# First-pass stores of split weights over GpSimd's DMA queue, in a kernel that converts later stages' weights in pairs of units

## The chip, the cores and the metric

One NeuronCore of one Trainium2 chip runs the kernel. The time is device microseconds of one execution, and the median of three is given. One more execution was profiled. Engines are called as the profile calls them: PE (TensorE matmul), PEld (its weight load), DVE (VectorE), ACT (ScalarE), POOL (GpSimd) and SP (SyncE, which here only issues DMAs).

## The reference

Attention over 4 batches of 12 heads (448 positions, head size 64, q and k normalised first), then two MLPs on the 1792 x 768 result.

```python
q_n, k_n = rmsnorm(q, g_q), rmsnorm(k, g_k)
scores = scale * np.matmul(q_n, k_n.transpose(0, 1, 3, 2))
attn = softmax(scores)                               # rows
x = np.matmul(attn, v)                               # -> 1792 x 768
y = ((x @ w_a) * (x @ w_b)) @ w_out                  # 768 -> 1536 -> 768
h = y @ w2_in                                        # 768 -> 2048
g = np.maximum(h, 0) + alpha * np.minimum(h, 0)
out = g @ w2_out                                     # 2048 -> 768
```

The five weight matrices come from HBM with 8 bytes an element.

## The kernel before

**Stages.** The MLPs run for each batch b as four stages: a (both first matrices, product of the two), y, h and o. The list `stages` begins a0 y0 h0 o0 a1 y1 ... The attention of the later batches is cut into small steps, and a rate per stage says how many steps are put between two units of weights. The attention of batch 0 runs alone before a0.

**Units.** A unit is 128 columns of a weight matrix. Every f32 product is made of three f16 products (high x high, high x low, low x high), so each weight is stored as a high and a low f16 half. The first time a unit is used it goes through four steps, some units ahead of its matmuls: `w_load` brings the 8-byte elements into `raw` (three buffers), `w_convert` makes f32 of them (`wf`, lines 806 to 820), `w_scale` finds a power of two from their squares (`tot`, `pw`), and `w_split` writes the halves into `w16` (three buffers; ACT writes the high half, DVE the low one). `w_split` also stores `w16` to HBM, to `sc_a`, `sc_y`, `sc_h` or `sc_o`; later stages of the same kind load the halves from there with no conversion (`w<-sc_a`, from about 425 us). Stage a stores each unit by itself (line 880, 24 stores of 384 KB); y, h and o store two units at a time (line 888).

**What else is on SP.** All loads of q, k, v and weights, the stores of lines 880 and 888, the stores of the result (line 1279), and the attention's transposes. For a pair of heads these are `qT` and `kT` (lines 354, 357), two copies `qS<-qT` (lines 360, 361) that wait for `qT` to land, and then seven `pT<-p` (line 489) of the probabilities. The matmuls `s<-kT,qT` and `s<-kT,qS` are the scores, `x<-pT,v` the product with the values. There is one buffer for `pT`: the first `pT` of a pair of heads waits until `x<-pT,v` of the pair before has read it.

**What sets the order.** A scheduler puts the instructions of each engine into one fixed order from the dependencies and its own estimates; each engine, and SP's queue, then runs its list in that order. An instruction that waits holds up all behind it on its engine. Matmuls of line 110 are all issued by one helper.

**POOL** has only a few small instructions before 392 us; later it loads and stores blocks from which combined weights are made (`form_block`, lines 673 and 705).

Of the kernel before, what the change touches and what calls it, by code (L numbers as in the profile page):

```python
# [19 lines left out]
def attention_gated_mlps_kernel(  # L20
# [15 lines left out]
    nc = tc.nc  # L36
# [676 lines left out]
    stream, pairs_of = [], []  # L713
# [8 lines left out]
    scratch, raws, wf, w16 = {}, {}, {}, {}  # L722
# [17 lines left out]
    def size(kind):  # L740
        return CHAINS[kind][2] * 128

    def views(t, n):
        return t.rearrange("p u l n -> p (u l n)")[:, 0:4 * n].rearrange("p (u l n) -> p u l n", u=2, l=2)

    def w_half():
        return wh_p.tile([128, 2, 2, 768], F16, tag="w16", name="w16")
# [118 lines left out]
    def w_split(u):  # L866
        if u not in scales:
            return
        t, s = wf.pop(u), scales.pop(u)
        n = size(stream[u][0])  # L870
        if stream[u][0] == "a":
            w = half16.pop(u) if u in half16 else views(w_half(), n)
            if u in members:
                half16[u + 1] = w
            w16[u] = w = w[:, u % 2]
            nc.scalar.activation(out=w[:, 0], in_=t, func=AF.Copy, scale=s)
            nc.vector.scalar_tensor_tensor(
                out=w[:, 1], in0=t, scalar=s, in1=w[:, 0], op0=ALU.mult, op1=ALU.subtract
            )
            nc.sync.dma_start(out=scratch[stream[u]], in_=w)  # L880
            return
        w = views(w_half(), n)
        t = t.rearrange("p (u n) -> p u n", u=2)
        nc.scalar.activation(out=w[:, :, 0], in_=t, func=AF.Copy, scale=s)
        nc.vector.scalar_tensor_tensor(  # L885
            out=w[:, :, 1], in0=t, scalar=s, in1=w[:, :, 0], op0=ALU.mult, op1=ALU.subtract
        )
        nc.sync.dma_start(out=whole[stream[u]], in_=w)
        for j, x in enumerate(members[u]):
            w16[x] = w[:, j]  # L890


    STEPS = [(w_load, 10), (w_convert, 8), (w_scale, 6), (w_split, 3)]
    AGAIN = [(w_load, 4)]
    cur = [0]
# [528 lines left out]
```

## Time and profile before

| | |
|---|---|
| runs | 1214.96, 1218.82, 1220.37 us; median 1218.82 |
| profiled execution | 1218.45 us, of which the span of the profile is 1216.5 us |
| busy in the span | PE 94%, DVE 67%, ACT 62%, PEld 54%, POOL 9% |
| DMA | 269.75 MB, mean 222 GB/s; SP's queue 246.40 MB, POOL's queue 22.10 MB |
| granted clock of PE | mean 0.983 of 2.4 GHz |

The span is the time between the first and the last instruction; the profiled execution is 1.95 us longer than it. PE is the engine with the least idle time, so its idle time and the stretches at half clock are where time can be won or lost.

### The profile page before, as it was taken

What the parts mean: (1) busy time and instruction counts of PE and PEld (TensorE: products, weight loads), DVE (VectorE), ACT (ScalarE), POOL (GpSimd) and SP (SyncE); (2) the same over time, 40 slices, a digit from 0 to 9 for tenths busy, and PEclk for the clock granted to TensorE, in tenths of its full rate; (3) what the DMA queues carried; (4) which work ended last, traced back from release to release, by engine and by line L of the source; (5) the groups of instructions that cost most, each with busy time, mean ns of one, the idle gap of its engine ahead of it and who ended that gap; (6) DMA issues with size and microseconds to landing.
All of it is one profiled execution on the core that took longest, in us unless ns stands there. A gap on an engine that the chain in (4) does not pass through costs nothing. (4 is left out here: it accounts for less than half of the span.)

```text
span 1216.5 us, 19623 instructions
## 1 busy us (share of the span) xinstructions
PE 1146.1 (94%) x7168; PEld 655.1 (54%) x7168; DVE 810.6 (67%) x1647; ACT 758.8 (62%) x1439; POOL 113.9 (9%) x176
## 2 busy tenths in 40 slices
PE   5997999799988899898999999999999999999997
PEld 3553555345544444444445554454555558996597
DVE  7888999789998764777745366554456677523631
ACT  6998999898998865667534366564245335513532
POOL 1000000000000100000012110122300572000000
PEclk9998999899999899999999999999999999999999
DMA  7557999999999999888794587798833797864455
GB/s 192 163 178 187 282 330 325 301 270 321 309 273 296 281 242 238 208 217 187 193 215 161 154 184 159 191 220 200 226 130 124 249 300 237 278 217 145 149 175 164
DMA packets 297280, 269.75 MB, mean 222 GB/s; under 512 B 176704, under 2 KB 261184, under 8 KB 297184
## 3 DMA queue, kind: packets, MB, share of 16 engines
q1 hardware_dynamic: 289392, 246.40, 74.2%
q0 software_dynamic: 7792, 22.10, 6.2%
q8 instruction: 56, 0.92, 0.3%
q14 instruction: 40, 0.33, 0.1%
HBM read 179.77 MB, written 43.25 MB: 183 GB/s over the span
## 5 line engine op out<-in xcount | busy, mean ns | idle before, releaser
L110 PEld LDWEIGHTS <-w 128*128 128x128 f16 x4776 | 463.0, 99 | 403.2 <-issue 52.2
L110 PE MATMUL p<-x,w 128*128 128x448 f16 x1728 | 338.5, 354 | 6.8 <-DVE ab L1141 4.6
L110 PE MATMUL p<-y,w 128*128 128x448 f16 x1152 | 221.0, 353 | 0.8 <-DVE y L952 0.8
L110 PE MATMUL p<-ab,w 128*128 128x448 f16 x648 | 129.4, 359 | 3.2 <-ACT ab L951 3.2
L110 PE MATMUL p<-g,w 128*128 128x448 f16 (+1 forms) x588 | 120.2, 359 | 2.9 <-DVE w L885 1.7
L483 DVE SCALAR_TENSOR_TENSOR p<-pf,ri,p 128x448 f16<-128x448 f32 x126 | 84.4, 681 | 38.9 <-ACT p L482 38.8
L482 ACT ACTIVATE p<-pf,ri 128x448 f16<-128x448 f32 x126 | 81.2, 664 | 43.1 <-DMA pT<-p 34.3
L420 DVE TENSOR_REDUCE nm<-s 128x2 f32<-128x896 f32 x84 | 91.1, 1085 | 22.3 <-PE s L110 22.3
L437 ACT ACTIVATE pf<-s,nm,esc 128x448 f32<-128x448 f32 x126 | 90.1, 719 | 1.5
L110 PEld LDWEIGHTS <-ws 128*128 128x128 f16 x714 | 68.5, 98 | 0.4
L1144 ACT ACTIVATE junk<-ab 128x448 uint8<-128x448 f32 x48 | 27.5, 573 | 58.8 <-DVE ab L1141 58.7
L806 ACT ACTIVATE wf<-raw 128x768 f32<-128x768 f32 (+2 forms) x50 | 57.7, 1165 | 8.0 <-DMA raw<-in_moe_w_out_dram 6.5
L812 DVE SCALAR_TENSOR_TENSOR wf<-raw,wf 128x768 int32<-128x768 int32 (+2 forms) x50 | 61.9, 1241 | 0.2
L705 POOL DMA_DIRECT2D f_o_S<-raw x48 | 33.9, 821 | 283.1 <-DVE raw L701 205.2
L820 ACT ACTIVATE junk<-wf 128x768 uint8<-128x768 f32 (+2 forms) x50 | 53.9, 1078 | 6.2 <-DVE wf L812 2.7
L110 PE MATMUL s<-kT,qT 128*64 128x448 f16 x252 | 47.7, 372 | 10.0 <-DMA kT<-k 7.4
L1141 DVE SCALAR_TENSOR_TENSOR ab<-p,inv_a,t 128x448 f32<-128x448 f32 x48 | 32.5, 677 | 26.5 <-PE p L110 26.2
L110 PE MATMUL s<-early 128*128 128x448 f32 x84 | 40.3, 602 | 9.8 <-ACT pf L437 9.2
L110 PE MATMUL l<-g,ws 128*128 128x224 f16 x480 | 49.6, 259 | 0.0
L110 PE MATMUL l<-g,w 128*128 128x224 f16 x480 | 49.4, 259 | 0.0
L673 POOL DMA_DIRECT2D raw<-sc_o x48 | 37.6, 986 | 121.2 <-DMA raw<-in_moe_w_out_dram 71.8
L110 PE MATMUL s<-kT,qS 128*64 128x448 f16 x252 | 46.4, 357 | 1.5 <-DMA qS<-qT 1.5
(175 smaller groups left out, 1529.0 us busy)
## 6 DMA issues: line engine op xcount, KB each, us to landing
w<-sc_a SPq DMA_DIRECT2D x36, 768.0 KB, 5.0
w<-sc_h SPq DMA_DIRECT2D x24, 768.0 KB, 4.3
raw<-in_moe_w_in_dram SPq DMA_DIRECT2D x16, 768.0 KB, 8.4
raw<-in_moe_w_out_dram SPq DMA_DIRECT2D x24, 512.0 KB, 6.9
raw<-in_moe_w_a_dram SPq DMA_DIRECT2D x12, 768.0 KB, 6.2
raw<-in_moe_w_b_dram SPq DMA_DIRECT2D x12, 768.0 KB, 6.9
sc_a<-w SPq DMA_DIRECT2D x24, 384.0 KB, 6.8
raw<-in_moe_w_out_dram SPq DMA_DIRECT2D x12, 768.0 KB, 9.0
```

Of the source, the lines that this page charges most:

```text
L110: nc.tensor.matmul(out=o, lhsT=a, rhs=b, start=first, stop=last)
L420: nc.vector.tensor_reduce(out=nm, in_=ps[:, :, 0:S], axis=AX.X, op=ALU.max, negate=True)
L437: nc.scalar.activation(out=pf, in_=ps[:, j, 0:S], func=AF.Exp, bias=nm[:, j:j + 1], scale=scale[j], accum_out=su[:, j:j + 1],)
L482: nc.scalar.activation(out=t[:, 0, :, 0:KP], in_=pf, func=AF.Copy, scale=r)
L483: nc.vector.scalar_tensor_tensor(out=t[:, 1, :, 0:KP], in0=pf, scalar=r, in1=t[:, 0, :, 0:KP], op0=ALU.mult, op1=ALU.subtract,)
L673: tc.keep_in_program_order(nc.gpsimd.dma_start(out=x[:, q], in_=s))
L705: nc.gpsimd.dma_start(out=formed[kind, i, name, j][:, :, cols], in_=d["x"][:, q])
L806: nc.scalar.activation(out=t, in_=hi.bitcast(F32), func=AF.Prelu, scale=2.0 ** -112, alpha=-(2.0 ** 32))
L812: nc.vector.scalar_tensor_tensor(out=ti, in0=lo, scalar=29, in1=ti, op0=ALU.logical_shift_right, op1=ALU.bitwise_or)
L820: nc.scalar.activation(out=junk(1536, t.shape[1]), in_=t, func=AF.Square, accum_out=sums[0][:, j:j + 1])
L1141: nc.vector.scalar_tensor_tensor(out=ab, in0=ps, scalar=i, in1=t, op0=ALU.mult, op1=ALU.mult)
L1144: nc.scalar.activation(out=junk(1536, S), in_=ab, func=AF.Square, accum_out=ssab[:, b % 2, f:f + 1],)
```

## The change

The store at line 880 is issued by POOL in place of SP. Its source, its destination and its size are the same.

```diff
@@ -877,7 +877,7 @@  in w_split
             nc.vector.scalar_tensor_tensor(
                 out=w[:, 1], in0=t, scalar=s, in1=w[:, 0], op0=ALU.mult, op1=ALU.subtract
             )
-            nc.sync.dma_start(out=scratch[stream[u]], in_=w)
+            nc.gpsimd.dma_start(out=scratch[stream[u]], in_=w)
             return
```

The 24 stores stand on POOL between its load of `al` and its first `cum` operation, with nothing between them. Since the scheduler makes a new order, other instructions change places too: on PE between rows 95 and 3315 of some 13000, that is from about 117 us to about 445 us; behind that the order is the same.

The first place is SP's queue at the end of a0. The rows before, where `raw_2519` is the last unit of `w_out` and `pT_2290` belongs to the attention of batch 1:

```order
L880 DMA sc_a22_0_1976<-w16_2417 128x1536
L888 DMA sc_y0_0_2079<-w16_2492 128x3072
L778 DMA raw_2519<-in_moe_w_out_dram 128x6x128
L489 DMA_TRANSPOSE pT_2290<-p16_1_110 128x8x128
L489 DMA_TRANSPOSE pT_2290<-p16_2_111 128x8x128
L778 DMA raw_2519<-in_moe_w_out_dram 128x6x128
L489 DMA_TRANSPOSE pT_2290<-p16_3_112 128x8x128
```

The same place in the changed kernel:

```order
L366 DMA vn_3773<-in_v_dram 112x2x256
L778 DMA raw_2519<-in_moe_w_out_dram 128x6x128
L888 DMA sc_y0_0_2079<-w16_2492 128x3072
L778 DMA raw_2519<-in_moe_w_out_dram 128x6x128
L778 DMA raw_2690<-in_moe2_w_in_dram 128x6x128
L888 DMA sc_y1_0_2178<-w16_2602 128x3072
L489 DMA_TRANSPOSE pT_2290<-p16_1_110 128x8x128
```

The second half of `raw_2519` stood behind two `pT`; it now stands ahead of them.

The second place is SP's queue in y0. Before, `qT_2975` and `kT_2978` (the next pair of heads) stood behind the last `pT_2290` and behind the first two `pT_2933`:

```order
L489 DMA_TRANSPOSE pT_2290<-p16_3_112 128x8x128
L778 DMA raw_2858<-in_moe2_w_in_dram 128x6x128 x2
L888 DMA sc_y4_0_2445<-w16_2917 128x3072
L778 DMA raw_2953<-in_moe2_w_in_dram 128x6x128 x2
L489 DMA_TRANSPOSE pT_2933<-p16_0_109 128x8x128
L489 DMA_TRANSPOSE pT_2933<-p16_1_110 128x8x128
L354 DMA_TRANSPOSE qT_2975<-q16_2836 128x7x128
L357 DMA_TRANSPOSE kT_2978<-k16_2838 128x8x112
```

In the changed kernel they come ahead of the last two `pT_2290`:

```order
L489 DMA_TRANSPOSE pT_2290<-p16_1_110 128x8x128
L778 DMA raw_2764<-in_moe2_w_in_dram 128x6x128 x2
L354 DMA_TRANSPOSE qT_2975<-q16_2836 128x7x128
L357 DMA_TRANSPOSE kT_2978<-k16_2838 128x8x112
L206 DMA kr_2987<-in_k_dram 112x2x256
L210 DMA qr_2986<-in_q_dram 128x448
L360 DMA qS_2980<-qT_2975 64x896
L361 DMA qS_2980<-qT_2975 64x896
L778 DMA raw_2858<-in_moe2_w_in_dram 128x6x128
L489 DMA_TRANSPOSE pT_2290<-p16_2_111 128x8x128
L888 DMA sc_y3_0_2359<-w16_2823 128x3072
L489 DMA_TRANSPOSE pT_2290<-p16_3_112 128x8x128
```

Two more pairs are moved in the same way, ahead of the first two `pT` of their own heads: `qT_4073` in o0 and `qT_4854` at the end of o0. On PE, the scores and the `x<-pT,v` around them stand earlier by 3 to some 30 matmuls of weights.

The third place is PE in o0, at the unit `w_4468`. Before, 21 matmuls of that unit, the 24 of `x<-pT,v_4081` and two more of the unit stood ahead of the first score of the next heads:

```order
L110 MATMUL x<-pT,v_4081 64x448
L110 LDWEIGHTS w_4468
L110 MATMUL p<-g_13_3903,w_4468 128x448
L110 LDWEIGHTS w_4468
L110 MATMUL p<-g_15_3989,w_4468 128x448
L110 LDWEIGHTS qT
L110 MATMUL s<-kT,qT 64x448
```

In the changed kernel the 24 come first, then 12 matmuls of the unit, and then eight scores in a row:

```order
L110 MATMUL p<-g_14_3947,w_4468 128x448
L110 LDWEIGHTS qT
L110 MATMUL s<-kT,qT 64x448
L110 LDWEIGHTS qT
L110 MATMUL s<-kT,qT 64x448
L110 LDWEIGHTS qS
L110 MATMUL s<-kT,qS 64x448
```

The scores moved ahead of 11 matmuls; on SP the items ahead of this `qT` and `kT` are the same ones as before.

## Rows read from the trace of the kernel before

**Rows 1.** The page, busy time of each engine.

```profile
PE 1146.1 (94%) x7168; PEld 655.1 (54%) x7168; DVE 810.6 (67%) x1647; ACT 758.8 (62%) x1439; POOL 113.9 (9%) x176
```

**Rows 2.** Stretches: length, busy time per engine, granted clock, DMA share, GB/s.

```profile
120.00:210.00 90.00, 90.00 (x523) 48.74 (x519) 85.89 (x188) 87.78 (x166) 0.00 (x0) 1.00 1.08 306
...
200.00:220.00 20.00, 16.35 (x108) 8.90 (x105) 16.85 (x25) 17.17 (x26) 0.00 (x0) 1.00 1.05 318
220.00:240.00 20.00, 14.83 (x63) 7.42 (x63) 15.97 (x32) 16.61 (x29) 0.19 (x1) 0.74 1.11 313
...
400.00:420.00 20.00, 16.60 (x86) 7.83 (x83) 13.47 (x25) 14.13 (x26) 0.60 (x1) 0.83 1.14 272
```

**Rows 3.** Line 880: issues (ns min/median/max, first and last start), landing.

```profile
L880 SPq DMA_DIRECT2D sc_a<-w x24: 339/527/3517, 87.6 to 201.9; - x24
...
DMA to landing us min/median/max: 2.8/6.8/12.1
```

**Rows 4.** Timeline of PE in a0: start, length, line, instruction, count.

```profile
138.35 3.56 PE L110 MATMUL p<-x,w 128*128 128x448 f16 x18
```

**Rows 5.** Timeline of POOL, first instruction after its loads at the start.

```profile
223.70 0.19 POOL L1286 TENSOR_TENSOR cum<-ix,iab 128x1 f32<-128x1 f32 x1 [214.24 <-DVE iab L123]
```

**Rows 6.** Line 673, POOL's loads: ns min/median/max, first and last start.

```profile
L673 POOL DMA_DIRECT2D raw<-sc_o x48: 720/989/1299, 392.8 to 951.2; - x48
```

**Rows 7.** Timeline of SP's queue around the end of a0.

```profile
201.87 3.52 SPq L880 DMA_DIRECT2D sc_a<-w  x1
205.48 0.38 SPq L888 DMA_DIRECT2D sc_y<-w  x1
...
214.46 3.36 SPq L489 DMA_TRANSPOSE pT<-p  x2
217.87 0.58 SPq L778 DMA_DIRECT2D raw<-in_moe_w_out_dram  x1
```

**Rows 8.** Timeline of ACT before y0; in brackets idle time and its releaser.

```profile
223.49 1.58 ACT L806 ACTIVATE wf<-raw 128x1536 f32<-128x1536 f32 x1 [1.65 <-DMA raw<-in_moe_w_out_dram]
...
225.66 1.78 ACT L951 ACTIVATE ab<-ab,sab 128x448 f16<-128x448 f32 x3
```

**Rows 9.** Timeline of PE at four places from y0 to o0.

```profile
226.38 2.02 PE L110 MATMUL p<-ab,w 128*128 128x448 f16 x5 [3.18 <-ACT ab L951]
...
256.84 2.46 PE L110 MATMUL x<-pT,v 112*64 112x448 f16 x24 [0.56 <-DVE pw L117]
...
267.02 0.38 PE L110 MATMUL s<-kT,qT 128*64 128x448 f16 x2 [1.42 <-DMA kT<-k]
...
404.21 0.58 PE L110 MATMUL s<-kT,qT 128*64 128x448 f16 x2 [3.40 <-DMA kT<-k]
```

**Rows 10.** PE's waits, 240 to 445 us: total, times, longest.

```profile
PE s L110 <- DMA kT<-k: 7.4, 4, 3.4
...
PE s L110 <- DMA qS<-qT: 1.5, 2, 0.9
```

**Rows 11.** Timeline of SP's queue in y0.

```profile
242.50 2.66 SPq L489 DMA_TRANSPOSE pT<-p  x1
...
259.33 2.62 SPq L489 DMA_TRANSPOSE pT<-p  x2
262.00 1.49 SPq L354 DMA_TRANSPOSE qT<-q  x1
263.54 1.29 SPq L357 DMA_TRANSPOSE kT<-k  x1
...
266.75 0.59 SPq L361 DMA_DIRECT2D qS<-qT  x1
```

**Rows 12.** Landing of `kT`, 250 to 445 us (five transposes).

```profile
DMA to landing us min/median/max: 3.0/3.4/8.8
```

**Rows 13.** Landing of `pT`, 230 to 260 us (five transposes).

```profile
DMA to landing us min/median/max: 4.9/6.4/10.5
```

## The prediction

> **What bounds the kernel now.** I read the page's busy times first, then the stretches, then PE's timeline at the edges of stages and PE's waits, and last SP's queue, which the change empties. PE is busy 94% of the span [rows 1], so at most some 70 us of idle time and a few stretches at half clock can be won back. In the stretches the reader is to see two different pieces. From 120 to 210 us, which is a0 and holds most of the 24 stores, PE is busy 90.00 of 90.00 us at full clock, with DVE at 85.89, ACT at 87.78 and a DMA share of 1.08 [rows 2]: all four are full, and PE has no gap that a freer queue could close. From 200 us on there are gaps, and behind a long one the clock falls: 0.74 over 20 us at the start of y0 is 10.4 us at the lower level of 1.2 GHz, and 0.83 in o0 is 6.8 us [rows 2]. PE's timeline shows what it waits for there: ACT's split of `ab` for 3.18 us before y0, `kT` for 1.42 us in y0 and for 3.40 us in o0 [rows 9]. In all, scores wait for `kT` 7.4 us in four places and for `qS` 1.5 us in two [rows 10]. These are transfers of SP's queue, so their place in it matters.
>
> **The store itself.** Removed from SP: 24 issues of 0.527 us in the median [rows 3], about 12.6 us of SP's time between 87.6 and 201.9 us. What covers it is a0's PE row without a gap, so I count 0. If that cover were gone, an SP item behind a store would come 0.5 us earlier, or 3.52 us at the last one, and the 24 together can give no more than SP's own time. Added to POOL: 24 issues. The nearest rows are POOL's own loads, 0.72 to 1.30 us each [rows 6], so 17 to 31 us of work on an engine that stands idle for 214.24 us up to 223.70 us [rows 5]; it queues nothing behind it but the tiny `cum`. I count 0. The bytes are the same, so I leave the DMA share as it is. Who reads the stores: `w<-sc_a` from 425 us, 220 us later, so landing time is no matter. Who waits for their end: the next writer of the `w16` buffer. Three buffers of two units turn over once in six units, and a unit is 18 matmuls in 3.56 us [rows 4], so in 21 us. A store now lands within 12.1 us at worst [rows 3]; one on POOL may land some 5 us later than that with nobody waiting. 0.
>
> So the store is worth nothing by itself, and the time moves by what the new order does. I price four places.
>
> **A, the start of y0.** Before, ACT waited 1.65 us for the last load of `w_out` ahead of the first split of `ab` [rows 8], because the second half of that load was issued at 217.87 us, behind two `pT` that came at 214.46 us [rows 7]. In the new order it stands right behind `sc_y`, which came at 205.48 us [rows 7], some 12 us earlier, so it has landed by then. That gives 1.65 us at most, since PE's first matmul of y0 waits for that split [rows 9]. Against it, two squarings of the next q and k now stand on ACT ahead of the last `ab` square and may eat part or all. Bounds 0 and -1.65; I take -1.0, nearer to the wait whose releaser is named.
>
> **B, scores that waited for `kT` and `qS`.** In y0, in o0 and at the end of o0, `qT` and `kT` were queued behind two `pT` of the next heads, which are held until PE has read `pT`: in y0 they went out at 259.33 us and `kT` only at 263.54 us [rows 11], landing 3.4 us later [rows 12], when PE had stood still for 1.42 us [rows 9]. In the new order `qT` and `kT` go ahead of these `pT`. Of the 7.4 and 1.5 us [rows 10], all but the 3.40 us of the fourth place [rows 9] belong to these three places: 7.4 - 3.4 + 1.5 = 5.5 us. The end is -5.5. The other end is 0, because PE's order has the scores earlier too, by up to some 30 matmuls of 0.2 us [rows 4], so that the gap may only change its place. I take half, -2.8.
>
> **C, values behind the transposes in y0.** What was taken forward pushes something back: the last two `pT` of y0's heads are now behind `qT`, `kT`, two loads and two `qS`. In the trace these took SP from 262.00 us to the end of the second `qS`, 266.75 + 0.59 = 267.34 us [rows 11], so 5.3 us, the wait of the first `qS` for `qT` to land among them. The last `pT`, issued at 242.50 us [rows 11], then goes out at 247.8 us. It lands 6.4 us later in the median, 10.5 us at most [rows 13]: at 254.2 or 258.3 us. `x<-pT,v` stood at 256.84 us [rows 9] and is 7 matmuls earlier, 7 x 0.2 = 1.4 us [rows 4], so it asks at 255.4 us, or at 254.4 us if A comes in. Bounds: 0 by the median landing, and +3.9 by the longest. I take +0.5, near the median, since it is within 0.2 us of being late.
>
> **D, the fourth place, o0.** SP's items ahead of this `kT` are the same, and it took 8.8 us to land, the longest of the five [rows 12]. PE arrives 11 matmuls earlier, 11 x 0.2 = 2.1 us [rows 4], and then stands still 2.1 us longer: +2.1. Bounds: 0 if `kT` lands in the usual 3.4 us, which would even take the 3.40 us away, and +3.8 if the half-clock stretch behind it grows from 6.8 to the 10.4 us seen at y0, half of the difference being lost.
>
> **The sum.** -1.0 - 2.8 + 0.5 + 2.1 = -1.2 us, against the profiled execution's 1218.45 us (its span of 1216.5 us and 1.95 us around it): 1217.2 us. That execution lies 0.4 us below the median of the runs, so the forecast for the median is 1217.6 us, given as 1217.5.
>
> **The rivals.** First, the freed queue does more than I count (faster): B gives its whole 5.5 us, A its 1.65 us, C and D nothing. Then 1218.8 - 7.2 = 1211.7 us, and if `kT` of o0 lands in 3.4 us too, 3.4 us of waiting and half of 6.8 us at half clock go as well: 1204.9 us. For it speaks that four of PE's six waits on these transfers have one cause, their place on SP; against it that the DMA share stays above 1.0 in all these stretches [rows 2], so that transfers sent earlier meet others.
>
> Second, and on the other side, C decides (slower). If the last `pT` of y0 lands as late as the slowest of the five, PE waits 3.9 us in one piece and the clock falls behind it as it did behind the waits of 3.18 and 3.40 us [rows 9], at a price of 3.4 to 5.2 us (half of 6.8 or 10.4 us). With A, B and D as above that is 1217.6 - 0.5 + 3.9 + 3.4 to 5.2 = 1224.4 to 1226.2 us. [...] For it speaks that the new order asks for values and scores earlier while the transfers have not become faster.
>
> Third, the stores starve on POOL (slower). In a0 DVE is busy 95% of the time [rows 2]. If POOL got to write a store only between DVE's instructions, stores would pile up, `w16` buffers would not come free, and ACT, then PE, would stop from the point where a store lands 17 us or more after its issue. One such stop per buffer turn of 21 us, five turns, at some 4 us: about 1238 us. Against it, POOL's loads take 0.72 us at best and never over 1.30 us, though many of them run beside DVE work [rows 6]. The Trainium skill, SBUF - State Buffer, section "SBUF: two separate sides", names this mechanism: while DVE runs an instruction that takes both of its ports, GpSimd cannot write the descriptors of its DMAs. By that rule the 24 stores would be late; no row here shows how late.
>
> **How the numbers follow.** A measurement of this kernel can tell about 0.5% from no change, 6.1 us; three runs before spread over 5.4 us. The likeliest case is my sum, with its own range of 1213 to 1224 us: 0.46. The first rival has 0.27, the second 0.23, the third 0.04. So faster by over 0.5% 0.27, within 0.5% 0.46, slower 0.27. The range of 1207 to 1228 us takes in the likeliest case, most of the first rival and the second, and leaves out its ends and the third.
>
> **What the changed profile would show.** The store: 24 issues of line 880 on POOL at 0.7 to 1.3 us, and a0 still without a gap on PE; a gap at a writer of `w16` would show the third rival. A: no wait of ACT line 806 on its load just ahead of the first `ab`. B: no wait of scores on `kT` or `qS` in y0, at 360 to 370 us and at 435 to 445 us. C: a wait of `x<-pT,v` on `pT` in y0. D: a wait on `kT` in o0 of 5 to 6 us in place of 3.40. I would be wrong if a long gap with half clock behind it appears or goes away: each is worth some 7 us, as much as all else together.

## The result and the profile after

The changed kernel takes 1222.80 us (median of 20 runs, 1217.54 to 1229.72), the kernel before 1216.45 us beside it (20 runs, 1212.71 to 1222.31). The ratio is 1.0052, with a 95% interval of 1.0035 to 1.0069: slower by about 6.3 us. The forecast was 1217.5 us, which was 1.2 us below the 1218.82 us that three runs of the kernel before had given, so it was a change too small to be measured. The profiled execution has a span of 1220.5 us, 4.0 us more than that of before: the profiles show the greater part of the loss, not all of it.

The page and the stretches that answer to [rows 1] and [rows 2] (length, busy time of PE, PEld, DVE, ACT and POOL, granted clock, DMA share, GB/s):

```profile
PE 1143.9 (94%) x7168; PEld 656.2 (54%) x7168; DVE 809.8 (66%) x1647; ACT 758.0 (62%) x1439; POOL 126.5 (10%) x200
```

```profile
120.00:210.00 90.00, 87.93 (x510) 47.98 (x511) 82.36 (x184) 85.45 (x161) 10.27 (x19) 1.00 1.09 311
200.00:220.00 20.00, 14.57 (x84) 7.72 (x83) 15.33 (x23) 16.12 (x26) 0.00 (x0) 0.83 1.09 344
220.00:240.00 20.00, 10.16 (x45) 5.24 (x42) 13.28 (x26) 14.06 (x25) 0.19 (x1) 0.66 1.11 290
400.00:420.00 20.00, 15.11 (x81) 7.69 (x79) 11.87 (x24) 12.82 (x25) 0.00 (x0) 0.83 1.16 230
```

PE's busy time is 2.2 us less in a span that is 4.0 us longer, so its idle time grew by 6.2 us: PE waits more. The stretch from 200 to 240 us, in which the passage from a0 to y0 lies, has lost 6.5 us of PE's busy time against [rows 2] (31.18 before, 24.73 now). The stores themselves answer to [rows 3]:

```profile
L880 POOL DMA_DIRECT2D sc_a<-w x24: 540/540/557, 85.4 to 197.1; - x24
```

Each issue costs POOL 0.54 us, below the 0.72 to 1.30 us that the prediction took from [rows 6], and the landing, the time from an issue to the arrival of its last byte, is 3.3/6.3/9.6 us (min, median, max) where it was 2.8/6.8/12.1.

**Where the time went.** I cut the span at rows of ACT's timeline that every kernel has: the first, sixth and twelfth `t<-p,inv_a` of a0 (line 1138), the first split of `ab` (line 951), the first `t` of a1. For the changed kernel three of these rows are:

```profile
164.41 0.61 ACT L1138 ACTIVATE t<-p,inv_a 128x448 f32<-128x448 f32 x1
...
213.50 0.63 ACT L1138 ACTIVATE t<-p,inv_a 128x448 f32<-128x448 f32 x1
...
232.15 4.02 ACT L951 ACTIVATE ab<-ab,sab 128x448 f16<-128x448 f32 x7
```

so the second half of a0 is 213.50 - 164.41 = 49.09 us and the passage to y0 is 232.15 - 213.50 = 18.65 us. In the kernel before, the twelfth `t` and, from [rows 8], the first split stand at 211.70 and 225.66 us:

```profile
211.70 0.62 ACT L1138 ACTIVATE t<-p,inv_a 128x448 f32<-128x448 f32 x1
```

The whole span, cut in this way:

| us | before | after | difference |
|---|---|---|---|
| start to first `t` | 128.5 | 126.7 | -1.8 |
| first half of a0 (1st to 6th `t`) | 37.80 | 37.72 | -0.1 |
| second half of a0 (6th to 12th) | 45.42 | 49.09 | +3.7 |
| passage to the first split of `ab` | 13.96 | 18.65 | +4.7 |
| y0, h0, o0, to the first `t` of a1 | 214.94 | 210.86 | -4.1 |
| a1 to the end | 775.94 | 777.48 | +1.5 |

The two losses show as two waits of PE in its timeline (start, length, line; in brackets idle time and what ended it):

```profile
213.53 4.31 PE L110 MATMUL x<-pT,v 112*64 112x448 f16 x24 [5.43 <-DVE pw L117]
...
228.48 0.60 PE L110 MATMUL tot<-ssab,ones 128*128 128x12 f32 x2 [7.20 <-ACT junk L1144]
...
232.87 7.30 PE L110 MATMUL p<-ab,w 128*128 128x448 f16 x25 [2.04 <-ACT ab L951]
```

In the kernel before, the first two waits were 1.85 and 1.80 us (the third was 3.18 us, [rows 9]):

```profile
211.97 2.46 PE L110 MATMUL x<-pT,v 112*64 112x448 f16 x24 [1.85 <-DVE pw L117]
...
219.67 0.39 PE L110 MATMUL tot<-ssab,ones 128*128 128x12 f32 x2 [1.80 <-ACT junk L1144]
```

Behind the first wait the granted clock of the changed kernel is at its lower level of 1.2 GHz (0.83 in the mean of 200 to 220 us): the 24 `x<-pT,v` take 4.31 us, before 2.46 us. What `pw` waited for stands in DVE's timeline, and, one step further, in ACT's:

```profile
208.93 0.96 DVE L809 TENSOR_SCALAR wf<-wf 128x1536 int32<-128x1536 int32 x1 [3.02 <-ACT wf L806]
...
211.60 1.81 DVE L885 SCALAR_TENSOR_TENSOR w<-wf,sc,w 128x1536 f16<-128x1536 f32 x1
213.33 0.15 DVE L117 TENSOR_SCALAR pw<-tot 128x1 int32<-128x1 int32 x1
```

```profile
207.31 1.58 ACT L806 ACTIVATE wf<-raw 128x1536 f32<-128x1536 f32 x1 [2.04 <-DMA raw<-in_moe_w_out_dram]
...
227.20 0.67 ACT L482 ACTIVATE p<-pf,ri 128x448 f16<-128x448 f32 x1 [5.94 <-DMA pT<-p]
```

In the kernel before, ACT stood at neither of these two places:

```profile
205.72 1.62 ACT L806 ACTIVATE wf<-raw 128x1536 f32<-128x1536 f32 x1
...
219.53 0.65 ACT L482 ACTIVATE p<-pf,ri 128x448 f16<-128x448 f32 x1
```

So the first wait of PE goes back to a late load of `w_out`, the second to a late `pT`. That `pT` is the first of three in SP's queue:

```profile
211.75 2.13 SPq L778 DMA_DIRECT2D raw<-in_moe_w_in_dram  x1
213.97 2.99 SPq L888 DMA_DIRECT2D sc_y<-w  x1
217.87 9.00 SPq L489 DMA_TRANSPOSE pT<-p  x3
```

It lies behind one of the two loads of `raw_2690` (768 KB) and a store of 768 KB and lands 9.3 us after its issue, when ACT has waited 5.94 us at line 482; the last sum of squares of `ab` (line 1144) stands behind that on ACT.

### The profile page after: what moved, and what is told of

Read it like the earlier page. It is cut to its first block, busy times and chain, and to the rows that moved or that the text cites. A ratio compares the mean times of both kernels' runs of the same rounds, so it can differ in the third digit from the quotient of the medians.

```text
span 1220.5 us, 19678 instructions
## 1 busy us (share of the span) xinstructions
PE 1143.9 (94%) x7168; PEld 656.2 (54%) x7168; DVE 809.8 (66%) x1647; ACT 758.0 (62%) x1439; POOL 126.5 (10%) x200
## 5 line engine op out<-in xcount | busy, mean ns | idle before, releaser
L110 PE MATMUL x<-pT,v 112*64 112x448 f16 x432 | 46.1, 365 | 7.3 <-DVE pw L117 6.4
```

The lines of the kernel that those rows point to most:

```text
L110: nc.tensor.matmul(out=o, lhsT=a, rhs=b, start=first, stop=last)
```

## The experiments

Two theories to begin with. "Order": the scheduler's new order lost the time, in the passage to y0. "Ring": the stores on a second queue make SP's transfers late in any order. To part them I write out a whole order: behind the kernel's last instruction every instruction of PE, DVE, ACT and SP is tied to the one ahead of it in a list taken from the built program of before ("old order") or of after ("new order"); the tie is meant to fix the order of issue and to add no wait. A kernel that has the ties and nothing else was not run; f4 below is the nearest to it, with a0 as in the kernel before and a ratio of 1.0015 (0.9995 to 1.0035).

```python
for row in ROWS:                       # one list for each engine
    for a, b in zip(row, row[1:]):
        tc.add_manual_dep(traced[b], a, NoSync, reason="order")
```

All kernels in one table; the ratio is to the kernel before, run beside it, and the stretches are those of the table above, from one profiled execution each.

| kernel | last 12 stores | order | median us | ratio (95%) | 2nd half of a0 | passage | to a1 |
|---|---|---|---|---|---|---|---|
| before | SP | old | 1216.45 | 1 | 45.42 | 13.96 | 214.94 |
| after | POOL | new | 1222.80 | 1.0052 (1.0035, 1.0069) | 49.09 | 18.65 | 210.86 |
| e1 | POOL | old | 1226.06 | 1.0078 (1.0056, 1.0101) | 49.70 | 15.18 | 211.56 |
| e2 | SP | new | 1219.14 | 1.0029 (1.0013, 1.0045) | 45.64 | 20.90 | 210.82 |
| e3 | POOL | new, `pT` ahead | 1221.35 | 1.0042 (1.0025, 1.0059) | 48.49 | 13.50 | 213.97 |
| g1 | SP | new, `pT` ahead | 1220.95 | 1.0037 (1.0018, 1.0056) | 46.60 | 16.92 | 215.59 |
| e4 | POOL | old, new from y0 | 1230.65 | 1.0133 (1.0107, 1.0160) | 52.81 | 15.28 | 227.50 |
| f3 | SP | old, new from 288 us | 1222.10 | 1.0052 (1.0032, 1.0073) | 45.39 | 13.39 | 224.79 |
| f1 | POOL, halves | old | 1231.27 | 1.0131 (1.0110, 1.0152) | 50.90 | 15.32 | 216.75 |
| f2 | POOL, halves | new | 1231.46 | 1.0110 (1.0068, 1.0151) | 48.30 | 18.51 | 210.29 |
| f4 | SP, first 12 POOL | old | 1218.61 | 1.0015 (0.9995, 1.0035) | 45.55 | 14.00 | 212.89 |
| g2 | POOL, first 12 SP | old | 1222.24 | 1.0061 (1.0037, 1.0085) | 53.49 | 15.41 | 213.66 |
| g3 | 6 POOL, 6 SP; first 12 POOL | old | 1225.79 | 1.0081 (1.0055, 1.0106) | 49.99 | 15.66 | 216.05 |
| g4 | POOL, 16 of 768 columns | old | 1220.38 | 1.0042 (1.0023, 1.0062) | 45.64 | 13.32 | 213.81 |
| h1 | ACT, first 12 SP | old | 1222.13 | 1.0059 (1.0038, 1.0079) | 52.97 | 13.03 | 212.27 |
| h3 | as h1, 5 us later | old | 1222.07 | 1.0056 (1.0035, 1.0077) | 51.05 | 14.41 | 211.69 |
| h2 | SP, first 12 POOL | its own | 1222.52 | 1.0051 (1.0028, 1.0073) | 45.67 | 14.05 | 221.80 |

### Queue and order apart: e1, e2

```diff
-            nc.sync.dma_start(out=scratch[stream[u]], in_=w)
+            nc.gpsimd.dma_start(out=scratch[stream[u]], in_=w)   # e1: lists of before
...
+        hold(tc, nc)                                             # e2: line 880 of before, lists of after
```

> The 24 stores are issued by POOL; every other instruction of PE, DVE, ACT and SP stands in the order of the kernel before. Theory 'order' (the time was lost by the new order at the end of a0, where ACT waited 5.94 us for a pT): that wait is gone, the first split of ab comes at about 224 to 226 us in place of 232.15, and the median is 1212 to 1217 us. Rival 'ring' (stores on a second queue slow SP's transfers in any order): the wait for raw and pT stays, and the median is 1220 to 1224 us.

> The 24 stores are back on SP, each behind the item it stood behind in the kernel before; every other instruction of all engines stands in the order of the changed kernel. Theory 'order': the loss at the end of a0 stays, first split of ab at 230 us or later, median 1221 to 1226 us. Rival 'ring': without the second queue the loss goes, median 1214 to 1218 us.

My theory "order" fell in e1: with the stores on POOL and nothing else moved the kernel is slower by 0.78%, more than the changed kernel. The new order alone costs 0.29%. Its loss is where "order" put it (passage 20.90 us), the queue's is elsewhere, in the second half of a0. Neither median fits a theory as it was written: 1226.06 us is above both ranges of e1, 1219.14 us lies between the two of e2. Two cautions belong to these numbers. e1's profiled execution is near the low end of its six runs, and its span is 4.6 us longer than that of before where the medians differ by 9.6 us; so the 4.3 us in the second half of a0 are about half of its loss, and where the rest goes isn't shown. And the two costs don't add up: by the medians the stores on POOL cost 9.6 us in the old order but 3.7 us in the new one (1222.80 against 1219.14).

In e1's SP queue one `pT` there takes 9.33 us to be issued and a load behind whose landing ACT waits comes late:

```profile
163.57 0.37 SPq L778 DMA_DIRECT2D raw<-in_moe_w_a_dram  x1
163.99 3.26 SPq L778 DMA_DIRECT2D raw<-in_moe_w_b_dram  x1
167.29 9.33 SPq L489 DMA_TRANSPOSE pT<-p  x1
```

```profile
180.15 0.90 ACT L806 ACTIVATE wf<-raw 128x768 f32<-128x768 f32 x1 [1.98 <-DMA raw<-in_moe_w_b_dram]
```

What the DMA engines did from 163.5 to 177 us in e1, by queue (packets, MB, share of 16 engines):

```profile
q1 hardware_dynamic: 2181, 1.57, 61.7%
q0 software_dynamic: 399, 1.97, 38.9%
```

and from 162 to 176 us in the kernel before, where q1 carries everything:

```profile
q1 hardware_dynamic: 4738, 4.07, 113.4%
```

In before, four stores were issued there, 4 x 384 KB = 1.57 MB, which leaves about 2.5 MB for loads and transposes. In e1 SP's loads and transposes got 1.57 MB through, while 1.97 MB of stores went beside them, and the sum came slower as well (264 GB/s for 292).

The packet records of the two traces show what was held up. A `pT` moves as 1024 packets of 256 bytes. The one that runs at 162 us took 2.4 us in before, from its first packet to its last; in e1 it took 9.2 us, with 249 packets of stores among its own, and for 4.9 us of that time, from 163.6 us on, no packet of a load started. With no store beside it, as at 192 us in e1, a `pT` takes 1.0 us. The one of 162 us takes 4.0 us in f4, 7.8 in g3, 9.3 in f1 and 10.4 in e4 (all described below). So in the old order the stores of the second queue stretch a transpose, and SP's loads wait behind it. In the changed kernel's own order this is weaker: the two transposes that are stretched most, at 144 and 186 us, take 5.5 and 4.1 us where e2 has 3.2 and 2.2 us, but the loads of the weights land after 10.8 us in the median (120 to 205 us) where e2 has 8.6 us.

### Two items of SP's queue: e3, g1

```diff
+L489 DMA_TRANSPOSE pT_2290<-p16_1_110   (and the two of p16_2, p16_3)
 L778 DMA raw_2690<-in_moe2_w_in_dram    (half)
 L888 DMA sc_y1_0_2178<-w16_2602
-L489 DMA_TRANSPOSE pT_2290<-p16_1_110   (and the two of p16_2, p16_3)
```

> The changed kernel in its own order, but for two items of SP: one half of raw_2690 (384 KB) and the store sc_y1 (768 KB) stand behind the three pT of the last heads in place of ahead of them. If these two items make the first pT land late (9.3 us after its issue), it lands some 4 us earlier, ACT's wait of 5.94 us falls to about 1 to 2 us, and the median is 1217 to 1219.5 us. If the first pT is late only because PE reads the old pT late (it is issued at 217.87 us, 3.4 us later than before), the wait stays at 5 to 6 us and the median at 1222 to 1224 us.

> As e2 (stores on SP, new order), with half of raw_2690 and the store sc_y1 behind the three pT, as in e3. From the last t of a0 to the first split of ab the kernel before took 13.96 us, e2 20.90 and e3 13.50; from there to the first t of a1 the old order took 214.94 us, the new one 210.8 to 210.9. If these add up, the boundary costs 13.5 to 14 us, the stretch behind it 211 to 214 us, and the median is 1211 to 1215 us, below both kernels. If what is won at the boundary is lost behind it (e3 took 213.97 us there), it is 1215 to 1219 us.

The item of `raw_2690` is 768 KB, not the 384 KB of the expectation. In e3 the cause of the changed kernel's second loss is shown: the wait at line 482 falls from 5.94 us to 0.54 us, and the passage from 18.65 to 13.50 us.

```profile
223.58 0.67 ACT L482 ACTIVATE p<-pf,ri 128x448 f16<-128x448 f32 x1 [0.54 <-DMA pT<-p]
```

But the median gains only 1.5 us, inside the intervals and short of the range expected: y0 to o0 takes 3.1 us longer than in the changed kernel. g1, the version that was to beat both, missed its numbers too (1220.95 us for 1211 to 1215). There the two items account for 4.0 of e2's long passage (20.90 to 16.92 us), but the same wait is still 3.45 us (7.2 in e2), for a reason that I did not find, and y0 to o0 takes 215.59 us. Passage and y0 to o0 together are 228.9 us in before and 225.3 to 232.1 us in the eight other kernels that keep the old order there, 227.5 to 232.5 us in the five of the new order. So what the new order saves behind y0 it does not save on top.

### Old order first, then the new: e4, f3

The lists of before up to the first matmul of y0 (e4) or to 288 us (f3), then those of after.

> Stores on POOL; all engines in the order of the kernel before up to the first matmul of y0, and in the order of the changed kernel from there on. Theory 'order': no loss at the end of a0, and scores no longer wait for kT and qS between 240 and 445 us (8.9 us in the kernel before), so 1208 to 1214 us. Rival 'ring': 1218 to 1222 us. A third way: what is won in y0 and o0 is lost again behind them (as the changed kernel's lead shrank after 445 us), 1215 to 1217 us.

> Stores on SP, all engines in the order of the kernel before up to 288 us of its trace (stage h0), then in the order of the changed kernel. If the new order is bad only around the start of y0 and good behind it (e2 stood 8 us behind the kernel before at 313 us and 2 us ahead at 523 us), the median is 1208 to 1214 us. If the lead is lost behind 523 us in any case, 1214 to 1218 us.

Both missed, and both have a wait at the seam. In f3 two loads of `vn`, which the new order has much earlier, come first behind it on SP, and their squares first on ACT:

```profile
293.74 0.63 ACT L374 ACTIVATE sq<-vn 112x512 f32<-112x512 f32 x1 [8.91 <-DMA vn<-in_v_dram]
```

PE waits 8.4 us there. In e4 the same kind of square holds ACT for 8.1 us, and its second half of a0 is as long (52.81 us) as in the other kernels with the last stores on POOL. Neither tells whether the new order would be better behind 288 us; a passage without such a seam was not run.

### Which stores, and how many: f4, g2, g3

```diff
-            nc.gpsimd.dma_start(out=scratch[stream[u]], in_=w)
+            (nc.gpsimd if u < 12 else nc.sync).dma_start(...)   # f4; g2: the reverse; g3: u < 18
```

> As e1, but only the first 12 stores (to about 145 us) are on POOL; the last 12 are on SP in their old places. Theory 'share' with a loss where SP's loads are late anyway (e1 lost 1.3 us up to 128 us and 5.5 us from 175 us on): 1216 to 1220 us. If the loss lies in the first half, or comes from SP's list without stores as such: 1222 to 1226 us.

> Old order, first 12 stores on SP, last 12 on POOL: the other half of f4. Theory 'overtaking' (stores of their own queue go ahead of loads that they stood behind on SP, and the loads of the last w_out units come late): the second half of a0, from the 6th to the 12th t, takes 48.5 to 50 us (e1 49.70, f4 45.55), and the median is 1222 to 1227 us. If the loss needs all 24 on POOL: 45.5 us and 1216 to 1219 us.

> Old order, first 18 stores on POOL, the last 6 on SP in their old places, three of them behind raw_2358. Theory 'overtaking': most of the loss is in the last 6, so the second half of a0 takes 45.5 to 47 us, x<-pT,v at its end waits about 1.9 us as in the kernel before and not 4.4 to 5.4 us, and the median is 1216 to 1220 us. If any store on POOL costs the same: about three quarters of e1's loss, 48 to 49 us and 1222 to 1225 us.

The first 12 stores (86 to 154 us in f4's trace, not up to 145 us) cost nothing that can be measured (1.0015, 0.9995 to 1.0035) and leave a0 as it was. The last 12 alone make its second half 53.49 us. The DMA share alone doesn't tell the two halves apart: in before it is 1.06 from 120 to 145 us and 1.09 from 145 to 205 us. In g3 my narrower idea fell, that only the last six matter because they overtake the last loads of `w_out`: with these on SP the second half still takes 49.99 us and `x<-pT,v` still waits 4.2 us.

### The bytes or the issues: g4

```diff
+            if u == 0:                       # 12 full stores into the arrays of units 12 to 23
+                ...
+            m = n if u < 12 else 16
-            nc.gpsimd.dma_start(out=scratch[stream[u]], in_=w)
+            nc.gpsimd.dma_start(out=scratch[stream[u]][:, :, 0:m], in_=w[:, :, 0:m])
```

> As e1 (all stores issued by POOL, old order), but each of the last 12 stores moves only 16 of its 768 columns. Left out are the other columns of these 12 units: their arrays hold the first unit's weights, put there by 12 full stores at about 87 us, so the later stages work on other numbers in the same way. If the bytes of the stores beside SP's transfers are the cause, the second half of a0 takes 45 to 45.6 us in spite of POOL's issues. If the issues on POOL, or SP's list without the stores, are the cause, it takes 48.5 us or more. The median is not to be read for itself, since the extra stores change the start of a0.

The second half of a0 falls to 45.64 us, with all 24 issues still on POOL and SP's list still without stores. So the issues on POOL and SP's list without stores do not cost the time by themselves; it takes the bytes of the last 12 stores. That these bytes cost it beside SP's transfers, and not in SP's own line, comes from before and f4, which move the same bytes on SP and have 45.42 and 45.55 us. One reservation: g4 leaves these bytes out altogether, and from 165 to 211 us its DMA engines move 257 GB/s (322 in before), so a cost of the issues that shows only beside full DMA engines would not be seen in it.

In the old order the longest landing of a `pT` between 120 and 205 us goes with the loss. In e1 (all 24 on POOL; min, median, max):

```profile
DMA to landing us min/median/max: 3.5/6.9/15.3
```

and in g4:

```profile
DMA to landing us min/median/max: 3.2/8.2/11.7
```

It is 9.5 us in before and 10.4 in f4, 15.4 in g2 and 15.7 in g3. In the new order it does not part the kernels: it is 9.5 us in e2 and 12.1 in h2, which lose nothing in the second half of a0, and 11.9 in the changed kernel and 11.2 in e3, which do. What parts them there is the median landing of the weights' loads: 8.6 and 9.0 us against 10.8 and 10.7.

### Packet length, and another queue: f1, f2, h1, h3

f1 and f2 store each unit as two column halves; h1 and h3 issue the last 12 stores on ACT's queue.

```diff
-            nc.gpsimd.dma_start(out=scratch[stream[u]], in_=w)
+            for c in range(2):                                      # f1, f2
+                at = slice(c * n // 2, (c + 1) * n // 2)
+                nc.gpsimd.dma_start(out=scratch[stream[u]][:, :, at], in_=w[:, :, at])
...
+            (nc.sync if u < 12 else nc.scalar).dma_start(...)       # h1, h3
```

> As e1 (stores on POOL, all other engines in the order of the kernel before), but each store is made as two column halves, so that its runs are 768 bytes long in place of 3072. Theory 'share': DMA engines that serve both queues in turn give the store's long packets most of their time (in e1 the stores moved 1.97 MB and all of SP's transfers 1.57 MB between 163.5 and 177 us); with runs as short as those of SP's loads SP gets more, and the median falls from 1226 to 1217 to 1222 us. Rival 'bytes': only the bytes in flight beside SP's count, 1224 to 1228 us.

> The changed kernel in its own order, with each store made as two column halves on POOL (runs of 768 bytes). Theory 'share': the raw loads land sooner than their median of 10.8 us, the wait of 5.4 us of x<-pT,v on DVE shrinks, and the median is 1216 to 1220 us (the time of e2, 1219, is the mark: same order with the stores on SP). Rival 'bytes': 1221 to 1225 us.

> As g2 (old order, first 12 stores on SP), but the last 12 stores are issued by ACT on its own queue, each at the place where its data are ready, in place of POOL. If any second queue beside SP's costs the time, the second half of a0 takes 49 to 54 us again (g2 53.49) and x<-pT,v waits over 3 us. If it is POOL's queue with its packets of 6144 bytes at some 260 ns (SP's store packets are 3072 bytes at 126 ns), the second half takes 45.5 to 46.5 us plus what ACT's issues cost, which the profile shows (12 x 0.1 to 0.5 us).

> As h1, but each of the last 12 stores stands some 5 us later in ACT's list. In h1 one store at 191.19 us, which had to wait until a raw load of SP landed, held ACT for 7.10 of the 7.55 us that the second half of a0 was longer. If that wait goes, the second half shows what a second queue of SP's own kind (packets of 3072 bytes) costs: 45.5 to 46.5 us if it costs nothing, so that g2's loss belongs to POOL's queue; 48.5 us or more, without a wait of ACT for its own stores, if any second queue costs it.

The packet records from 85 to 210 us, by size:

| kernel, queue | packets of the stores | mean of one | engine time of the stores / 16 |
|---|---|---|---|
| before, SP (128 more packets lie outside) | 2944 of 3072 bytes | 126 ns | 23.2 us |
| e1, POOL | 1536 of 6144 bytes | 257 ns | 24.7 us |
| f1, POOL | 1536 of 4608, 768 of 3072 bytes | 252, 132 ns | 30.6 us |
| h1, ACT (12 stores) | 1536 of 3072 bytes | 126 ns | 12.1 us |
| SP's other packets, in e1 | 18817 of 1024, 12544 of 256 bytes | 55, 30 ns | |

The halves did not become short packets, so f1 and f2 are no test of packet length, and both medians lie above both of their ranges. In the old order the halves cost more, 1.31% for 0.78%; they differ from e1 in their engine time (30.6 for 24.7 us) and in the number of issues (48 for 24), which no run parts. f2's profiled execution, with a span of 1218.1 us at the low end of its runs, does not show where its median of 1231.46 us loses.

h1 and h3 did not settle whether any second queue costs this. In both, the profile names an earlier transfer of SP as what ACT waited for just behind one of its own stores; in h1:

```profile
191.19 0.33 ACTq L880 DMA_DIRECT2D sc_a<-w  x1
191.56 0.72 ACT L437 ACTIVATE pf<-s,nm,esc 128x448 f32<-128x448 f32 x1 [7.10 <-DMA raw<-in_moe_w_out_dram]
```

and in h3:

```profile
196.67 0.33 ACTq L880 DMA_DIRECT2D sc_a<-w  x1
197.09 0.58 ACT L1144 ACTIVATE junk<-ab 128x448 uint8<-128x448 f32 x1 [4.70 <-DMA qT<-q]
```

Of h1's 7.55 us and h3's 5.63 us in the second half of a0 these waits (7.10; 4.70 and one of 0.82) leave 0.5 and 0.1 us. That would make POOL's queue the costly one if the transfers waited for had not themselves been late. But in h1 a `pT` takes 6.6 us, from 181.3 us on, with 252 packets of ACT's stores among its own (the same one takes 1.2 us in before), and the longest landing of a `pT` is 15.7 us, as with the stores on POOL; in h3 that landing is 10.8 us. So ACT's queue stretched SP's transfers too, at least in h1, and the question stays open: a kernel without these waits was not run.

### The harmless half in an order of its own: h2

The edit of f4, with nothing tied.

> First 12 stores on POOL, last 12 on SP, and the scheduler's own order for this program, nothing pinned. If only the bytes of the last 12 beside SP's transfers cost time, the second half of a0 takes 45.4 to 45.7 us; the rest is the luck of the order it makes: 1212 to 1220 us.

The second half of a0 is 45.67 us, as f4's and as expected. The whole is slower by 0.51% all the same (1222.52 us for 1212 to 1220): y0 to o0 takes 221.80 us, and from 220 to 460 us scores wait for `kT` and `qS` for 9.4 + 4.6 = 14.0 us, where it was 8.9 us in [rows 10]. So the order that the scheduler finds around an edit that costs nothing measurable (f4) can cost as much as the change of this study.

No kernel here beats the kernel before.

## Why the prediction was wrong

**The store itself: the step that failed.** The prediction counted it at 0: the landing of a store is no matter, "The bytes are the same, so I leave the DMA share as it is." That share did stay (1.08 and 1.09), and the stores landed early enough. What the step left out is the landing of SP's loads and transposes beside them. On SP a store took its turn in one line with them; on POOL it goes through the same 16 DMA engines beside them, and those had a share of 1.08 already [rows 2]. Measured: +3.7 us in the second half of a0 in the changed kernel; +0.78% in e1, where nothing else changed, with one `pT` stretched from 2.4 to 9.2 us and the loads held behind it. That a0's PE row had no gap [rows 2] was read as cover; it only said that the loads were just early enough. The Trainium skill, DMA: Bandwidth & Descriptors, section "Queues, rings and completion order", says that an engine which has work from several queues takes a packet from each in turn. The trace agrees as far as it goes: in e1 both queues were served in the same 13.5 us, POOL's for 38.9% and SP's for 61.7% of the engines' time, with packets of 257 ns on the one and of 30 to 55 ns in the mean on the other; whether the profile's packets are those of the page, and how the turns went, no run shows. The prediction did not weigh this, and it speaks against the change.

**A, the start of y0: wrong sign.** The mechanism named did come: no wait for `raw_2519` stands ahead of the first split of `ab` any more. But the passage became longer by 4.7 us, not shorter by 1.0. I asked what `raw_2519` was moved ahead of, and not what else was moved ahead of the three `pT`: one load of `raw_2690` and `sc_y1`, which the rows of the new order showed. e3 shows that these two cost it (18.65 to 13.50 us). The first loss handed on is a small part at most: the first `pT` can go only when `x<-pT,v` has read the old one, but SP was busy with `sc_y1` until 216.96 us, 0.9 us before that `pT` went out; and e2, without the first loss, has an even longer passage (20.90 us).

**B, C and D: right in B, wrong in D, and not worth what they seemed.** From 240 to 445 us no score waits for `kT` or `qS` any more, the 3.40 us of D included, so B gave its whole waits and D went the other way: the transposes of `kT` landed within 5.4 us, where D had counted on the 8.8 us of [rows 12] again. (11 x 0.2 us is 2.2, not 2.1; that changes nothing.) PE's waits in that stretch (total, times, longest) now begin:

```profile
PE p L1276 <- ACT nm L433: 4.9, 1, 4.9
PE tot L110 <- ACT junk L820: 2.3, 3, 1.0
...
PE x L110 <- DVE pw L117: 1.0, 2, 0.6
```

C did not come: no `x<-pT,v` waits for `pT`, which landed within 7.8 us. The place of D's wait has a new one, 4.9 us at 411 us, because ACT stood for 5.45 us at a square of `vn` (line 374) that was not yet loaded. The stretch to a1 gained 4.1 us where B, C and D summed to -0.2. But e2, with the stores on SP, gains the same 4.1 us and is still slower than before by 0.29%, and in e3 and g1, which shorten the passage, most of that gain is gone. The forecast of -1.2 us for the new order was a miss of sign as well: +0.29%, some 3.5 us.

**The rivals.** The second, a late `pT` with half clock behind it, has the size: it lay 5.6 to 7.4 us above the time before, and 6.3 us were measured (its 1224.4 to 1226.2 us miss the 1222.80 us, since they start from the three runs). That is in part luck: its place was y0 and a wait of PE for `pT`, where nothing came; the late `pT` was one ahead of y0, on ACT, and gave the passage its 4.7 us, and the other loss was not in it at all. Its reading of the clock was loose too: in the kernel before the granted clock fell at 221.7 us, ahead of the wait of 3.18 us, and at 402.7 us, within the wait of 3.40 us; and from 348 to 352 us it is 0.57 in the mean, behind waits of 1.25 and 0.67 us. The third did not come: POOL issued each store in 0.54 us while DVE was busy for 82.36 of 90 us, and stores landed after 6.3 us in the median; so the rule named beside it (the Trainium skill, SBUF - State Buffer, "SBUF: two separate sides") decided nothing here, and no row shows whether a DVE instruction of a0 takes both ports. Its place, though, a cost of the stores on POOL in a0, was the right one. Of the first, the waits of B and D did go, but not its time.

What stays open: the +1.5 us behind a1 and the -1.8 us ahead of a0 are within what one execution differs from another; whether only POOL's queue, or any second one, costs the 3.7 us; why the first 12 stores cost nothing there; and where the medians lose what the single profiles do not show (2.3 us in the changed kernel, 5.0 us in e1).

## What to carry to other kernels

Here, with the 16 DMA engines full, moving stores to an idle engine's queue freed no transfer: it took each store out of the line in which it stood with the loads and transposes, and these paid. Ask of a moved transfer not only who waits for it, but whose transfers it now runs beside; an edit of bytes (g4) helps to tell that from the cost of the issue. And where a scheduler makes a new order, list everything that now stands ahead of each transfer that an engine waits for, and run the old order with the edit alone: here the order alone cost 0.29%, the edit alone 0.78%, and both together 0.52%.

## What was not expected of the hardware

The same list of instructions ran up to the first `t` of a0 in 128.5 us (before) and 124.7 us (f3), so one profiled execution can differ from another by 3.8 us there, as much as the first loss of the changed kernel; the stretches behind it repeat much better (37.39 to 38.24 us for the first half of a0 in all kernels but the two with halves). POOL's queue moved the stores in packets of 6144 bytes at 257 ns where SP's made 3072 bytes at 126 ns, with nearly the same engine time in all (24.7 us for 24 stores, 23.2 us for 23). And a `pT` that takes 1.0 us with no store beside it (e1, 192 us) took up to 10.4 us with the stores of another queue beside it (e4).
